# Windowed attention and a gated expert on one core: weights converted 1024 columns at a time, in borrowed memory

## The chip, the core and the metric

The kernel runs on one core of a Trainium2 chip. The core has a matrix engine (TensorE, PE in the rows; PEld is its loading of weights), a vector engine (VectorE, DVE), a scalar engine (ScalarE, ACT), a general one (GpSimd, POOL) and SyncE (SP), which here only issues DMAs. Each runs its own list of instructions in order, and they wait for each other through semaphores. The metric is the device time of one execution in microseconds; less is better. A profile is one more execution, taken by the hardware profiler.

## The reference

Eight batches of attention over 8 heads, 576 positions, 64 numbers a head. Then a gated expert with a convolution over the positions:

```
scores = q @ k.T / 8;  heads 0-3 see the last 32 positions,
                       heads 4-7 every 4th of the last 128
attn   = softmax(scores) @ v;  x = attn, heads side by side (576 x 512 a batch)
h      = relu(x @ w_in)                                   # 512 -> 1024
conv   = sum of conv_w[k] * h at position + k - 1,  k = 0..2
out    = (h * sigmoid(conv)) @ w_out                      # 1024 -> 512
```

All inputs and the output are fp32. The weights reach the device as raw 64-bit words, as the host has them, and are made into fp32 terms there.

## The kernel before

**Numbers.** An expert matmul runs in fp32r, one pass. So that its result is good enough, each operand is a sum of two terms, hi and lo, and a product is three matmuls: hi x hi, hi x lo, lo x hi (`TERMS`). This holds for x (`x0a`, `x0b` are hi and lo of one slot), for w_in (`wi`), for w_out (`wo`) and for the gated h (`g`).

**Attention.** A pair of heads is one attention block, four to a batch, 32 in all. One block is: 36 or 40 small score matmuls (L322, S below); maxima, exp and sums on VectorE and ScalarE; a transpose on VectorE (L369); 42 or 44 matmuls with v (L380, V below); and the copy of the result into hi and lo of x (L432 ScalarE, L435 VectorE). In the first seven blocks (`EASED`) TensorE adds the mask by matmuls (L309), and exp is nine small instructions (L346).

**Expert.** For each batch the first product (L460, E below) makes 16 units of 12 matmuls: 8 pieces of 128 columns of h, each in halves of 288 positions. ScalarE applies relu (L467). The gate of a piece is a scaled copy (L478), two taps (L472 VectorE), sigmoid (L483), the product (L485), and the split into hi and lo of g (L488, L490). The second product (L502, G below) takes blocks of 128 positions, 24 matmuls each, over the 8 pieces.

**Weights.** `weights` loads one chunk of 512 words (L529, half a MiB) and makes its terms. ScalarE takes the magnitude (L538), VectorE shifts it, adds the sign, cuts off the last bits and forms the rest (L540, L542, L545, L547). There are 8 chunks of w_in, 8 of w_out and one small one of conv_w. In ten of the 16 (`SUMMED`) lo comes from TensorE: identity times the main part, minus the rest, minus hi (L556 to L558, one after the other in a PSUM bank; this is called a correction below), and a copy out (L561). In the other six VectorE adds and subtracts (L563, L569).

**Order.** `Planner` writes all engines' orders. Every piece of work has an engine, a cost, a due number (`DUE`, `PAIR`, `WI`, `WO`, `EXTRA`, and `SHIFT` for single tasks), the tasks it comes after and the buffers it uses. At each step the planner takes the engine whose next work can start first by its costs, and among the work that can start within 0.25 of that, the one with the smallest due number. The order is then written out and kept. Where the plan leaves TensorE idle in its first 60 us, `filled` puts in filler matmuls of `ones` with itself (L600), whose result nobody reads. `ones` is the bf16 identity: GpSimd makes an fp32 identity, ScalarE copies it (L573), and the first filler waits for that.

**Buffers.** `qk` has two slots, `v` three, `u` ten, `g` eight (one for each 128 columns of h), and the conversion has four of raw words, three of terms (`w`) and two of rests (`r`). SP issues all loads in the planned order; a load whose slot is still read waits on SP, and what stands behind it waits too.

Of the kernel before, what the change touches and what calls it, by code (L numbers as in the profile page):

```python
# [8 lines left out]
F32 = mybir.dt.float32  # L9
# [27 lines left out]
    0: (508.06, 118.7, 1183.15, 74.57, 324.56, -13.54),  # L37
    1: (77.62, 987.7, -1760.76, 250.32, 1004.25, 273.69),
    2: (-1800.55, 209.28, 1068.97, 212.32, 742.18, 600.16),
    3: (430.32, 309.56, 279.83, 495.43, 968.39, -311.64),  # L40
    4: (-1333.76, -56.0, 788.64, 898.23, 629.43, 69.23),
    5: (-209.08, -1085.66, 3838.62, 239.71, 685.35, 49.23),
    6: (-1730.83, 900.6, 769.13, -1140.48, 291.43, -1030.59),
    7: (249.67, -1019.42, -1317.3, 803.1, 449.65, -1107.9),
}
PAIR = {
    0: (-1284.89, -2039.18, -1339.23, -1351.72),
    1: (-1032.27, -1049.19, -1041.5, -1122.07),
    2: (-994.96, -257.3, -37.45, -138.07),
    3: (88.07, -10.86, -134.77, 220.53),  # L50
    4: (646.12, 416.46, 324.57, 690.94),
    5: (847.1, 778.65, -227.72, 874.3),
    6: (752.11, 349.59, 1190.92, 1132.25),
    7: (3817.41, 1342.98, 1934.23, 391.1),
}
WI = (91.3, 189.33, 106.05, 82.13, -1680.2, -142.95, -815.76, 129.17)
WO = (-809.27, 346.83, 388.99, -762.3, 778.33, 873.39, 232.39, 1087.63)
EXTRA = (-1465.48, 232.79, -92.67, 599.5, 258.06, 231.57, 708.35, -1147.4, -1135.53, -1294.92, -1448.95,
    300.52, 3695.3, 609.75, 18.47, 85.79, -1136.82, 113.69, -959.95, -186.62, 253.06, 28.17, 459.74, -1675.04,
    1.22, -1061.9, 64.19, -192.43, -1248.75, -17.19, -998.69, 3818.85, 955.89, -1328.81, 709.92)  # L60

SHIFT = {
# [11 lines left out]
MASKS = 70.0  # L74


EASED = range(7)
EARLY = (0, 3)
SUMMED = (0, 1, 3, 4, 5, 6, 7, 11, 12, 14)
LEFT = 16  # L80
# [133 lines left out]
def attn_moe(ctx: ExitStack, tc: tile.TileContext, qk_p, qk_d, v_p, v_d, w_in, w_out, conv, mask, out):  # L214
# [306 lines left out]
    def weights(src, n, due, dst=None, pair=None, summed=False):  # L521
# [43 lines left out]
        if dst is not None:  # L565
            return last
# [126 lines left out]
```

## Time and profile before

| | us |
|---|---|
| three runs | 524.24, 525.31, 522.60; median 524.24 |
| profiled execution | 522.08 |
| its span, first to last instruction | 520.3 |
| TensorE busy | 507.4 |
| VectorE busy | 392.0 |
| ScalarE busy | 297.6 |
| DMA queue of SP | 51.10 MB, 29.8% of the span's capacity |

A busy share is an average over the whole span. The granted clock of TensorE is 1.00 of full speed in every slice. DMA is busy mainly in the first 60 us: the first slices of 13 us move 287, 372, 300 and 170 GB/s, later ones mostly under 150. VectorE is at 0.9 or more of most slices until about 170 us and at 0.2 or less in the last 50. The chain of work that ended last is followed back from the last instruction; a piece of it is a run of instructions of one line, with its start and its length, and what the engine waited for stands in it as DMA, another engine, or "issue" (nothing that the profile shows).

### The profile page before, as it was taken

The numbers are of one execution on the slowest core, as the hardware profiler recorded it, in microseconds if no ns is written. First come the engines' busy times: TensorE is split into PE (matmuls) and PEld (weight loads), VectorE is DVE, ScalarE is ACT, GpSimd is POOL, SyncE is SP. The second block draws the span as 40 slices with busy tenths as digits, with TensorE's granted clock in tenths as the row PEclk, the third lists the DMA queues.
The fourth block names the chain that finished last, engine by engine and source line by source line (L and its number), as shares of the span: only waits on it lengthen the run. The fifth ranks groups of instructions, "written<-read, shape, count | busy, mean of one in ns | idle before, by whom it ended". The sixth has DMA issues, their size and how long they took to land.

```text
span 520.3 us, 17211 instructions
## 1 busy us (share of the span) xinstructions
PE 507.4 (98%) x7700; PEld 440.7 (85%) x7700; DVE 392.0 (75%) x676; ACT 297.6 (57%) x637; POOL 1.4 (0%) x26
## 2 busy tenths in 40 slices
PE   5899999999999999999999999999999999999997
PEld 3568889998877998799977998899789988998885
DVE  5899899999989389999978589878876881772400
ACT  6955897667533487348741476765366632862410
POOL 1000000000000000000000000000000000000000
PEclk9999999999999999999999999999999999999999
DMA  8985643101364113532154113202420011001111
GB/s 287 372 300 170 222 153 117 37 1 41 105 213 144 53 54 87 192 125 64 39 176 144 64 54 125 94 1 70 152 72 1 1 43 42 21 2 40 42 41 59
DMA packets 17274, 52.33 MB, mean 101 GB/s; under 512 B 2096, under 2 KB 2480, under 8 KB 17200
## 3 DMA queue, kind: packets, MB, share of 16 engines
q1 hardware_dynamic: 17056, 51.10, 29.8%
q8 instruction: 60, 0.98, 0.8%
q10 hardware_dynamic: 144, 0.13, 0.1%
q14 instruction: 14, 0.11, 0.1%
HBM read 41.79 MB, written 9.44 MB: 98 GB/s over the span
## 4 chain that ended last, share of the span: by engine, by line
PE 96%; DMA 2%; ACT 1%; issue 0%; DVE 0%; SPq 0%; ACTq 0%
PE banks L502 40%; PE banks L460 39%; PE banks L380 7%; PE banks L322 6%; PE banks L600 2%; PE banks L556 1%; DMA qk<-in_qk_d_dram 1%; DMA qk<-in_qk_p_dram 1%; ACT s L346 1%; PE banks L557 0%; PE banks L558 0%; PE banks L309 0%; SPq L529 0%; DVE m L335 0%; ACT wi L561 0%
## 5 line engine op out<-in xcount | busy, mean ns | idle before, releaser
L472 DVE SCALAR_TENSOR_TENSOR u<-u,conv_sb,u 128x576 f32<-128x576 f32 x128 | 103.5, 817 | 31.2 <-ACT u L478 29.4
L467 ACT ACTIVATE u<-banks 128x288 f32<-128x288 f32 x128 | 51.3, 411 | 53.4 <-PE banks L460 53.2
L485 DVE TENSOR_TENSOR u<-u,u 128x576 f32<-128x576 f32 x64 | 47.8, 756 | 14.6 <-ACT u L483 14.1
L514 ACT COPY u<-banks 128x512 f32<-128x512 f32 (+1 forms) x36 | 20.7, 579 | 58.7 <-PE banks L502 57.7
L460 PE MATMUL banks<-x0a,wi 128*128 128x288 f32 x192 | 54.1, 298 | 0.0
L483 ACT ACTIVATE u<-u 128x576 f32<-128x576 f32 x64 | 42.8, 684 | 19.6 <-DVE u L472 19.3
L478 ACT ACTIVATE u<-u,conv_sb 128x576 f32<-128x576 f32 x64 | 49.6, 778 | 3.0 <-DVE u L485 1.9
L460 PE MATMUL banks<-x2a,wi 128*128 128x288 f32 x160 | 45.1, 299 | 0.0
L460 PE MATMUL banks<-x5a,wi 128*128 128x288 f32 x160 | 44.8, 295 | 0.0
L460 PE MATMUL banks<-x4a,wi 128*128 128x288 f32 x160 | 44.7, 294 | 0.0
L460 PE MATMUL banks<-x3a,wi 128*128 128x288 f32 x160 | 44.7, 298 | 0.0
L380 PEld LDWEIGHTS banks<-pt,v 32*64 32x64 f32 x2752 | 34.9, 131 | 10.8 <-issue 4.8
L380 PE MATMUL banks<-pt,v 32*64 32x64 f32 (+2 forms) x2752 | 38.7, 226 | 1.4 <-ACT wi L561 1.1
L322 PEld LDWEIGHTS banks<-qk 64*32 64x32 f32 x2432 | 28.8, 106 | 10.6 <-issue 4.1
L322 PE MATMUL banks<-qk 64*32 64x64 f32 x2432 | 34.2, 226 | 2.1 <-DMA qk<-in_qk_d_dram 0.9
L460 PEld LDWEIGHTS banks<-x0a,wi 128*128 128x128 f32 x192 | 36.0, 188 | 0.2
L360 ACT ACTIVATE s<-s 128x576 f32<-128x576 f32 x25 | 17.1, 686 | 28.2 <-DVE s L358 28.1
L460 PEld LDWEIGHTS banks<-x2a,wi 128*128 128x128 f32 x160 | 29.9, 188 | 0.8 <-ACT u L467 0.2
L460 PEld LDWEIGHTS banks<-x3a,wi 128*128 128x128 f32 x160 | 29.8, 188 | 0.6 <-ACT u L467 0.2
L460 PEld LDWEIGHTS banks<-x5a,wi 128*128 128x128 f32 x160 | 30.0, 188 | 0.2
L460 PEld LDWEIGHTS banks<-x4a,wi 128*128 128x128 f32 x160 | 30.0, 188 | 0.0
L502 PE MATMUL banks<-wo,g0a 128*128 128x512 f32 x72 | 29.1, 404 | 0.0
(139 smaller groups left out, 1283.3 us busy)
## 6 DMA issues: line engine op xcount, KB each, us to landing
qk<-in_qk_d_dram SPq DMA_DIRECT2D x16, 672.0 KB, 4.5
qk<-in_qk_p_dram SPq DMA_DIRECT2D x16, 592.0 KB, 4.7
out_dram<-u SPq DMA_DIRECT2D x31, 256.0 KB, 2.2
v<-in_v_p_dram SPq DMA_DIRECT2D x16, 384.0 KB, 3.6
v<-in_v_d_dram SPq DMA_DIRECT2D x16, 384.0 KB, 3.6
raw<-in_w_out_dram SPq DMA_DIRECT2D x8, 512.0 KB, 3.7
raw<-in_w_in_dram SPq DMA_DIRECT2D x8, 512.0 KB, 6.6
out_dram<-u SPq DMA_DIRECT2D x9, 128.0 KB, 2.3
```

The source lines that it names most:

```text
L322: nc.tensor.matmul(banks[quad * 32:quad * 32 + 32, at[bank], c * W:c * W + W], q, k, start=i == 0 and not eased, stop=i == len(parts) - 1, ...
L360: last = plan.add("ACT", 0.685, step[3], lambda: nc.scalar.activation(out=nine(s.t), in_=nine(s.t), func=AF.Exp, scale=SCALE), [last], [s] ...
L380: nc.tensor.matmul(banks[hd * 64:hd * 64 + 64, bank, o:o + n], v.t[quad * 32:quad * 32 + 32, block // 2, block % 2 * 64:block % 2 * 64 + 6 ...
L460: nc.tensor.matmul(bank(ps)[:, 0:HALF], wi[jw][fc][:, k * 128:k * 128 + 128], x[k].t[jx][:, hf * HALF:hf * HALF + HALF], start=(k == 0 and ...
L467: relu.append(plan.add("ACT", 0.4, due + 1.6 * u + relued, lambda fc=fc, hf=hf, ps=ps: nc.scalar.activation(out=h[fc].t[:, 1 + hf * HALF:1 ...
L472: nc.vector.scalar_tensor_tensor(out=body(c[fc]), in0=h[fc].t[:, k:S + k], scalar=conv_sb[:, k, fc:fc + 1], in1=body(c[fc]), op0=ALU.mult, ...
L478: t = plan.add("ACT", 0.777, d, lambda fc=fc: nc.scalar.activation(out=body(c[fc]), in_=body(h[fc]), func=AF.Copy, scale=conv_sb[:, 1, fc: ...
L483: t = plan.add("ACT", 0.686, d + shaped, lambda fc=fc: nc.scalar.activation(out=body(c[fc]), in_=body(c[fc]), func=AF.Sigmoid), [t], [c[fc ...
L485: t = plan.add("DVE", 0.755, d + times, lambda fc=fc: nc.vector.tensor_tensor(out=body(c[fc]), in0=body(c[fc]), in1=body(h[fc]), op=ALU.mu ...
L502: nc.tensor.matmul(bank(ps), g[k].t[jg][:, col:col + 128], wo[jw][k], start=(k == 0 and i == 0), stop=(k == NF - 1 and i == 2))
L514: t = plan.add("DVE" if half else "ACT", 0.16 + 0.00093 * (c1 - c0), out_due + by_block * u + copied, lambda ps=ps, o=o, c0=c0, c1=c1, cop ...
L600: nc.tensor.matmul(banks[:, i], ones, ones.unsqueeze(1).to_broadcast([128, 4, 128]), start=True, stop=True)
```

## The change

Weights are loaded and converted in eight chunks of 1024 words (one MiB) and not sixteen of 512; one chunk holds two of the former, side by side, and the host's layout follows. A summed chunk is corrected in two halves on TensorE, as a bank holds 512. Four of the eight chunks are summed.

The conversion gets hardly any memory of its own. A `Slot` is a place with two lives: first fp32 scratch (`before`), then the final tile. Magnitude and rest of a chunk stand where its hi will be, and its main part where its lo will be, or in the one `w` where VectorE makes lo. The raw words of w_in are loaded into the places of g, which is not in use yet; those of w_out have one raw buffer. g has four places for pairs of chunks. u grows from 10 to 13.

GpSimd makes the bf16 identity directly and first, then the fp32 one. All eight blocks of the first two batches are eased, a third block's scores use the expert's banks (`EARLY`), and all due numbers are new, `SHIFT` is empty.

```diff
-    0: (508.06, 118.7, 1183.15, 74.57, 324.56, -13.54),
+    0: (1422.91, 1408.33, 435.35, 42.62, 1436.64, -870.71),
...
-EASED = range(7)
-EARLY = (0, 3)
-SUMMED = (0, 1, 3, 4, 5, 6, 7, 11, 12, 14)
+EASED = range(8)
+EARLY = (0, 3, 7)
+SUMMED = (1, 3, 5, 6)
...
-NU, NX, NR, NW, NT = 10, 7, 4, 3, 2
+NU, NX, NR, NW, NT = 13, 7, 1, 1, 2
...
-    wi = [[const.tile([128, 512], F32R, name=f"wi{j}{c}") for c in range(NF)] for j in range(2)]
-    wo = [[const.tile([128, DM], F32R, name=f"wo{j}{c}") for c in range(NF)] for j in range(2)]
+    twice = ctx.enter_context(tc.tile_pool(name="twice", bufs=1))
+
+    class Slot:
+
+        def __init__(self, name, shape, before):
+            self.name, self.shape, self.kept = name, shape, None
+            self.before = twice.tile(before, F32, name=f"{name}early", tag=name)
+
+        def __getitem__(self, at):
+            if self.kept is None:
+                self.kept = twice.tile(self.shape, F32R, name=self.name, tag=self.name)
+            return self.kept[at]
+
+    wi, wo = ([[Slot(f"{n}{j}{c}", [128, 1024], [128, 1024]) for c in range(NF // 2)] for j in range(2)] for n in ("wi", "wo"))
...
-    slots("g", NF, [128, S + REST], F32R, 2)
+    plan.pool("g", [Slot(f"g{i}", [128, 2, 2, S + REST], [128, 2048]) for i in range(NF // 2)])
...
-    def weights(src, n, due, dst=None, pair=None, summed=False):
+    def weights(src, n, due, pair, summed=False, words=None):
+
         f = n / 512
-        raw, u, t = Buffer("raw"), Buffer("w", 1), Buffer("w")
-        r = Buffer("r") if summed else u
-        both = lambda: raw.t[:, :2 * n].bitcast(I32).rearrange("p (n t) -> p n t", t=2)
+        hi, lo = pair
+        raw = words or (Buffer("raw") if n > 512 else None)
+        r, w = [Buffer("r")] if summed else [], [] if summed or n < 512 else [Buffer("w")]
+        u = lambda d=F32: (hi.before if n > 512 else hi).bitcast(d)
+        t = lambda d=F32: (w[0].t if w else lo.before if n > 512 else lo).bitcast(d)
+        both = lambda: (raw[0].t.before if words else raw[0].t if raw else conv_raw)[:, :2 * n].bitcast(I32).rearrange("p (n t) -> p n t", t=2)
...
-            part = plan.add("ACT", 0.62, due + EXTRA[22], lambda: nc.scalar.copy(out=hi, in_=words(t)), [main], [t])
+            part = plan.add("ACT", 0.16 + 0.465 * f, due + EXTRA[22], lambda: nc.scalar.copy(out=hi[:, :], in_=t()), [last])
...
+            halves, added = [slice(0, 512), slice(512, 1024)], []
+            pss = [Buffer("nn" if words else "mm") for _ in halves]
+            for at, ps in zip(halves, pss):
+                added.append(plan.add("PE", 1.43, due + EXTRA[23], lambda at=at, ps=ps: add(ps, at), [part, whole, negated], [*r, ps], "E"))
...
-    made = plan.add("POOL", 0.6, -1e4, lambda: make_identity(nc, ident))
-    made = plan.add("ACT", 0.29, -1e4, lambda: nc.scalar.copy(out=ones, in_=ident), [made])
-    plan.add("ACT", 0.29, -1e4, lambda: nc.scalar.mul(out=minus, in_=ident, mul=-1.0), [made])
+    made = plan.add("POOL", 0.6, -2e4, lambda: make_identity(nc, ones))
+    whole = plan.add("POOL", 0.6, -1e4, lambda: make_identity(nc, ident), [made])
+    negated = plan.add("ACT", 0.29, -5e2, lambda: nc.scalar.mul(out=minus, in_=ident, mul=-1.0), [whole])
...
+    wired = sum([weights(w_in[c], 1024, WI[c], (wi[0][c], wi[1][c]), c in SUMMED, gs[0][c]) for c in range(NF // 2)], [])
+    wored = sum([weights(w_out[c], 1024, WO[c], (wo[0][c], wo[1][c]), c + NF // 2 in SUMMED) for c in range(NF // 2)], [])
```

How this moves instructions is seen best in three places. The numbers behind names are the buffers' own in each program, and line numbers from L300 on differ by 1 to 7 between the two.

SP's first loads, before (the raw words of a chunk go to a `raw` buffer; 128x1024 words of four bytes are half a MiB):

```order
L529 DMA raw_156<-in_conv_dram 128x48
L529 DMA raw_157<-in_w_out_dram 128x1024
L571 DMA kinds_sb<-in_mask_dram 128x320
L294 DMA qk_99<-in_qk_p_dram 128x1184
L529 DMA raw_158<-in_w_in_dram 128x1024
L294 DMA qk_100<-in_qk_d_dram 128x1344
L529 DMA raw_159<-in_w_out_dram 128x1024
L294 DMA qk_99<-in_qk_d_dram 128x1344
L529 DMA raw_156<-in_w_in_dram 128x1024
L294 DMA qk_100<-in_qk_p_dram 128x1184
```

and after (`g0early` is g's place 0 in its first life):

```order
L576 DMA kinds_sb<-in_mask_dram 128x320
L535 DMA conv_raw<-in_conv_dram 128x48
L295 DMA qk_88<-in_qk_p_dram 128x1184
L295 DMA qk_89<-in_qk_p_dram 128x1184
L535 DMA g0early<-in_w_in_dram 128x2048
L297 DMA v_90<-in_v_p_dram 128x768
L295 DMA qk_88<-in_qk_d_dram 128x1344
L295 DMA qk_89<-in_qk_d_dram 128x1344
L297 DMA v_91<-in_v_p_dram 128x768
L535 DMA raw_135<-in_w_out_dram 128x2048
L295 DMA qk_88<-in_qk_d_dram 128x1344
L295 DMA qk_89<-in_qk_p_dram 128x1184
```

Four weight chunks of half a MiB stood among the first nine loads, two of them ahead of the second qk load. Now two qk loads come first, then one MiB of w_in, and the first chunk of w_out only behind four qk and two v loads.

TensorE around the first expert matmul, before (L556 to L558 are a correction, L460 E, L380 V, L600 a filler):

```order
L600 MATMUL banks<-ones 128x512
L556 MATMUL banks<-w_161,ident 128x512
L557 MATMUL banks<-r_163,minus 128x512
L558 MATMUL banks<-wi_72,minus 128x512
L460 MATMUL banks<-x2a,wi_70 128x288
L460 MATMUL banks<-x2b,wi_70 128x288
L460 MATMUL banks<-x2a,wi_78 128x288
L380 MATMUL banks<-pt_114,v_101 64x64 x24
L380 MATMUL banks<-pt_114,v_101 64x32 x8
L380 MATMUL banks<-pt_114,v_101 64x16 x8
L380 MATMUL banks<-pt_114,v_101 64x32 x4
L600 LDWEIGHTS ones
```

and after (the same are L559 to L561, L463, L381 and L607):

```order
L607 MATMUL banks<-ones 128x512
L559 MATMUL banks<-wi13early,ident 128x512
L560 MATMUL banks<-r_137,minus 128x512
L561 MATMUL banks<-wi_580,minus 128x512
L381 MATMUL banks<-pt_102,v_92 64x64 x24
L381 MATMUL banks<-pt_102,v_92 64x32 x8
L381 MATMUL banks<-pt_102,v_92 64x16 x8
L381 MATMUL banks<-pt_102,v_92 64x32 x4
L607 LDWEIGHTS ones
L607 MATMUL banks<-ones 128x512
L463 MATMUL banks<-x0a,wi_580 128x288
L463 MATMUL banks<-x0b,wi_580 128x288
```

Before, the correction above is the fifth, and the first three E stand between it and the fourth V block. After, the one above is the second half of the first chunk, and the third V block and a filler stand between it and the first E. Ahead of these rows there are 39 fillers before and 57 after.

VectorE in its first conversions, before (L540 to L547 are a chunk's steps, L335 to L339 the maxima of an S block):

```order
L540 TENSOR_SCALAR w_162<-w_162 128x512
L542 SCALAR_TENSOR_TENSOR w_160<-raw_157,w_162 128x512
L545 TENSOR_SCALAR w_162<-w_160 128x512
L547 SCALAR_TENSOR_TENSOR r_163<-raw_157,w_162 128x512
L335 TENSOR_REDUCE m_107<-banks 128x2x4
L337 TENSOR_REDUCE m_107<-banks 128x1
L339 TENSOR_SCALAR m_107<-m_107 128x9
L540 TENSOR_SCALAR w_161<-w_161 128x512
L542 SCALAR_TENSOR_TENSOR w_162<-raw_158,w_161 128x512
L545 TENSOR_SCALAR w_161<-w_162 128x512
L547 SCALAR_TENSOR_TENSOR r_164<-raw_158,w_161 128x512
```

and after (L546 to L550 the steps, L336 to L340 the maxima, L365 to L368 an S block's division):

```order
L336 TENSOR_REDUCE m_98<-banks 128x2x4
L338 TENSOR_REDUCE m_98<-banks 128x1
L340 TENSOR_SCALAR m_98<-m_98 128x9
L336 TENSOR_REDUCE m_96<-banks 128x2x4
L338 TENSOR_REDUCE m_96<-banks 128x1
L340 TENSOR_SCALAR m_96<-m_96 128x9
L546 TENSOR_SCALAR wi03early<-wi03early 128x1024
L548 SCALAR_TENSOR_TENSOR wi13early<-g0early,wi03early 128x1024
L365 TENSOR_SCALAR z_101<-z_101 128x9
L367 RECIPROCAL z_101<-z_101 128x9
L368 TENSOR_TENSOR s_95<-s_95,z_101 128x576
L550 TENSOR_SCALAR wi03early<-wi13early 128x1024
```

The maxima of four S blocks now stand ahead of the first weight chunk's first step, where two whole chunks stood around the first block's maxima.

## Rows read from the trace of the kernel before

**Rows 1.** The page: busy engines; DMA issues (count, KB each, us to landing)
```profile
PE 507.4 (98%) x7700; PEld 440.7 (85%) x7700; DVE 392.0 (75%) x676; ACT 297.6 (57%) x637; POOL 1.4 (0%) x26
...
qk<-in_qk_d_dram SPq DMA_DIRECT2D x16, 672.0 KB, 4.5
```

**Rows 2.** TensorE's waits, whole span: waiter, awaited, us in total, times, longest
```profile
PE banks L600 <- ACT ones L573: 5.8, 1, 5.8
PE banks L380 <- ACT wi L561: 1.1, 1, 1.1
PE banks L322 <- DMA qk<-in_qk_d_dram: 0.9, 1, 0.9
```

**Rows 3.** The chain that ended last: start us, us, what, instructions
```profile
2.12 5.23 DMA qk<-in_qk_p_dram
...
8.81 6.37 DMA qk<-in_qk_d_dram
...
21.78 2.91 PE banks L600 x13
24.69 0.86 PE banks L556 x2
25.55 0.23 PE banks L557
...
36.01 0.40 PE banks L460 x3
36.41 1.19 PE banks L380 x72
37.59 0.32 PE banks L600
37.91 1.98 PE banks L460 x15
...
40.55 0.65 issue
...
54.05 1.06 PE banks L322 x65
...
67.68 3.39 PE banks L460 x24
...
96.00 2.76 PE banks L502 x12
...
103.26 5.47 PE banks L502 x24
```

**Rows 4.** Timeline, 0 to 30 us: start, us, engine, line, operation
```profile
1.67 0.29 POOL masks.py:199 TENSOR_SCALAR_AFFINE_SELECT ident<-ident 128x128 f32<-128x128 f32 x1
...
3.10 0.18 DVE L542 SCALAR_TENSOR_TENSOR w<-raw,w 128x24 int32<-128x24 int32 x1
...
9.94 0.31 ACT L346 ACTIVATE s<-banks,m 128x64 f32<-128x64 f32 x1
...
12.47 0.24 ACT L346 ACTIVATION_READ_ACCUMULATOR s<-banks,m 128x1 f32 x1
```

**Rows 5.** Stretches: us, busy us of each engine, clock, DMA share, GB/s
```profile
20.00:25.00 5.00, 4.42 (x100) 2.73 (x100) 4.83 (x14) 5.00 (x25) 0.00 (x0) 1.00 1.00 400
50.00:84.00 34.00, 33.98 (x809) 30.20 (x807) 31.98 (x62) 29.67 (x85) 0.00 (x0) 1.00 0.56 180
```

**Rows 6.** VectorE by line and shape: count, busy us, mean ns, idle before
```profile
L472 DVE SCALAR_TENSOR_TENSOR u<-u,conv_sb,u 128x576 f32<-128x576 f32 x128 | 103.5, 817 | 31.2 <-ACT u L478 29.4
L485 DVE TENSOR_TENSOR u<-u,u 128x576 f32<-128x576 f32 x64 | 47.8, 756 | 14.6 <-ACT u L483 14.1
...
L542 DVE SCALAR_TENSOR_TENSOR w<-raw,w 128x512 int32<-128x512 int32 x16 | 11.0, 686 | 0.3
...
L540 DVE TENSOR_SCALAR w<-w 128x512 int32<-128x512 int32 x16 | 6.6, 416 | 1.8 <-ACT w L538 1.8
```

**Rows 7.** Timeline of VectorE, 112.9 to 115 us
```profile
113.02 2.27 DVE L472 SCALAR_TENSOR_TENSOR u<-u,conv_sb,u 128x576 f32<-128x576 f32 x3
```

More of the change, by code (lines that the diff above doesn't have):

```diff
@@ L544, in weights @@
-        main = last
-        last = step(0.265, [t, u], lambda: nc.vector.tensor_scalar(
-            out=ints(u), in0=ints(t), scalar1=-0x800000, scalar2=None, op0=ALU.bitwise_and))
-        rest = step(0.53, [raw, u, *([r] if summed else [])], lambda: nc.vector.scalar_tensor_tensor(
-            out=r.t if summed else words(r), in0=low().bitcast(U32), scalar=-2.0 ** -52 if summed else 2.0 ** -52,
-            in1=words(u), op0=ALU.mult, op1=ALU.mult))
-        if summed:
-            hi, lo = pair
-            ps = Buffer("nn")
-            part = plan.add("ACT", 0.62, due + EXTRA[22], lambda: nc.scalar.copy(out=hi, in_=words(t)), [main], [t])
-            def add():
-                nc.tensor.matmul(bank(ps), ident, words(t), start=True, stop=False)
-                nc.tensor.matmul(bank(ps), minus, r.t, start=False, stop=False)
-                nc.tensor.matmul(bank(ps), minus, hi, start=False, stop=True)
-            last = plan.add("PE", 1.43, due + EXTRA[23], add, [rest, part], [t, r, ps], "E")
-            return plan.add("ACT", 0.6, due + EXTRA[24], lambda: nc.scalar.copy(out=lo, in_=bank(ps)), [last], [ps])
@@ L562, in weights @@
-        last = rest
-        last = step(0.53, [t, r], lambda: nc.vector.tensor_tensor(
-            out=words(t) if dst is None else dst, in0=words(t), in1=words(r), op=ALU.add))
-        if dst is not None:
-            return last
-        hi, lo = pair
-        last = plan.add("ACT", 0.62, due + EXTRA[22], lambda: nc.scalar.copy(out=hi, in_=words(t)), [last], [t])
-        return step(0.53, [t], lambda: nc.vector.tensor_tensor(out=lo, in0=words(t), in1=hi.bitcast(F32), op=ALU.subtract))
+            out=u(), in_=high().bitcast(F32), func=AF.Abs, scale=2.0 ** -112), [last], raw)
@@ L592, in attn_moe @@
                          [masked[1]])
-    wired = [weights(w_in[c], 512, WI[c], pair=(wi[0][c], wi[1][c]), summed=c in SUMMED) for c in range(NF)]
-    conved = weights(conv, 3 * NF, -9e3, dst=conv_sb.rearrange("p t c -> p (t c)"))
-    wored = [weights(w_out[c], 512, WO[c], pair=(wo[0][c], wo[1][c]), summed=c + NF in SUMMED) for c in range(NF)]
+    gs[0] = [Buffer("g") for _ in range(NF // 2)]
+    flat_conv = conv_sb.rearrange("p t c -> p (t c)")
+    conved = weights(conv, 3 * NF, -9e3, (conv_u, flat_conv))
+    wired = sum([weights(w_in[c], 1024, WI[c], (wi[0][c], wi[1][c]), c in SUMMED, gs[0][c]) for c in range(NF // 2)], [])
+    wored = sum([weights(w_out[c], 1024, WO[c], (wo[0][c], wo[1][c]), c + NF // 2 in SUMMED) for c in range(NF // 2)], [])
     for b in range(B):
```

97 lines of the change are left out of this document (56 added, 41 removed), and 10 rows, old and new, of the table SHIFT.

## The prediction, made before the change was run

> **What bounds the kernel now.** I read the page's busy times first, then who waited for whom on TensorE, then the opening on the timeline, then the chain of work that ended last. TensorE is busy 507.4 of 520.3 us [rows 1]; the reader is to see there that little but TensorE's own work and its early waits is left to change. The longest wait is the 5.8 us before its first instruction, for the bf16 identity that ScalarE copies; the next are 1.1 us for a copy of weight terms and 0.9 us for a load [rows 2]. The last wait in the chain ends at 41.2 us ("issue" [rows 3]); from there on the chain is TensorE alone to the end. Inside TensorE's busy time three things are not the reference's work: 45 filler matmuls (L600), ten corrections of weights (L556 to L558), and the turns between kinds of matmul.
>
> So I compare the two programs by the time at which TensorE has done the same useful work. The scores (S), probability-value products (V), first (E) and second (G) expert products are the same number in both. Their prices are pieces of the chain [rows 3]: an S block 1.06 us; a V block 1.19; 15 E matmuls 1.98, so 0.132 each; 24 G matmuls 5.47, so 0.228 each; 13 fillers 2.91, so 0.224; one filler with the turn around it 0.32; one correction 0.86 + 0.23 + 0.23 = 1.32. After an S or V block the next E pays a turn: 24 E took 3.39 instead of 3.17. There are 64 returns from S or V in both orders, so the turns cancel.
>
> **The change part by part.**
>
> *The identity.* GpSimd's select of the first identity ends at 1.96 us [rows 4]; in the new order it writes the bf16 one first and no ScalarE copy lies between, so fillers start near 2 us instead of 5.8. That alone gives nothing: the first S needs its qk load. This landed at 7.35 (issued 2.12, 5.23 us later [rows 3]) behind 0.55 MB of w_out and conv words. Now only the mask and the conv words stand ahead of it: half a MB less, at 400 GB/s [rows 5], is 1.3 us, and its issue is one DMA earlier, 0.4 us. The first S starts at about 5.7.
>
> *The walk to the first E.* SP gives the loads of S1, S2, 1 MB of w_in and a v, and then waits in order: the third qk load until S1 has read its buffer, the fourth until S2 has. In the same place a qk load of before took 6.37 us from issue to landing [rows 3], and I take 6.4. S1 ends at 6.8; the load issued at 6.9 lands at 13.3. S2 ends at 8.6; the other lands near 15.2. The 17 fillers between are done at 12.7, so S3 runs from 13.3 to 14.5, S4 waits until 15.3 and ends at 16.5. The 18 fillers behind it end at 20.7; S5's load, issued at 14.6, lands at 21.0, and S5 ends at 22.1. Seven fillers; V1 ends at 25.0. Nine exps take 2.8 us (9.94 to 12.71 [rows 4]); those of S5 stand behind VectorE's maxima and V1's x terms, so they run from 27.2 to 30. V2 runs from 27.0 to 28.2, its x terms follow on ScalarE and VectorE until 31.5, V3 ends at 32.7, a filler waits there for the copy of the first correction, and the first E starts at 33.2. Before, it started at 36.0 [rows 3]. First term: -2.8 us. The uncertain number in it is the 6.4 us: at 5, S3 to S5 would be bounded by the fillers and the first E comes 2 us sooner; at 7.5 it comes 2 us later.
>
> *The corrections.* Ten of 512 columns become eight halves of 1024, 2 x 1.32 less in all. But before the first E there were five of the ten and now there are two of the eight (order rows): after it six remain against five. Second term: +1.3 us. The three fewer ahead of it are in the walk.
>
> *Fillers.* 62 for 45, but 57 of them stand before the first E and are in the walk. After it five remain against six. Third term: -0.3 us.
>
> *Width.* On VectorE a two-operand conversion step takes 0.69 us at 512 columns [rows 6] and 0.18 at 24 [rows 4]; 0.16 of it does not grow, and I estimate 1.21 at 1024; one-operand steps go from 0.42 to 0.66. Each pair of steps saves 0.16, on VectorE and ScalarE, which lie beside TensorE: directly I give it nothing. What it can cost is its grain: a TensorE block that waits for x, or an exp, stands behind a step of 1.2 us and not 0.7. From the walk after the first E: V5 waits 0.5 us for the x terms of V4, which stand behind three such steps; S7 waits 1.0 us for exps that follow a copy of 1024 weights; the long run of E waits 0.2 us for V8's x. That is 1.7 us, in place of the 0.65 us that before lost there ("issue" [rows 3]). Fourth term: +1.05 us. Its bounds are -0.65 (no wait left) and about +3 (each of these waits behind one step more).
>
> *The memory.* Raw words of w_in lie in g, terms in the place of the finished ones, and raw, w and r have one, one and two buffers. The one raw buffer makes SP wait for a conversion before each later w_out load, and loads of qk and v and stores queue behind it. The last of these waits is for VectorE's 172nd instruction, near 102 us; the qk loads of the next two S blocks are issued before it, and that is the cover. The g pieces are freed by pairs of chunks; every G block reads all of them anyway. The u buffers go from 10 to 13. I cost all this at nothing; without the cover one late S or V costs TensorE about its own length, 1 us.
>
> A rule of the Trainium skill ("DMA: Bandwidth & Descriptors", section Bandwidth) speaks for the wide loads: transfers should be batched to 1 MiB and more to come near peak, and the fit in its section on the anatomy of one DMA is 2.0 us plus the bytes at 436 GB/s. Estimated from that page, 16 weight loads would be 51 us of queue and 8 would be 35. By the row the queue moved 400 GB/s at a busy share of 1.00 with pieces of half a MiB [rows 5], so the fixed part is already hidden, and the sum takes nothing from it.
>
> *Later.* At the first G of the new order all corrections, 11 S, 8 V and 384 E are done. From 49.5 us, after S7, there are until then 336 E (44.5 us), four S, three V, four corrections, two fillers and seven turns, 59.9 us, and 0.2 of wait: 109.6. Before began G at 96 [rows 3] and mixed it with E. What is left behind that point is the same work in both, and before records no wait in it.
>
> Sum: -2.8 + 1.3 - 0.3 + 1.05 = -0.75 us. The profiled execution took 522.08 us, 1.8 around its span, so such an execution would take 521.3. The median of the runs is 524.24, 2.2 above the profiled one, and I forecast against the median: **523.5 us**. About 0.5%, 2.6 us, is what a measurement of this kernel can tell from no change.
>
> **The rivals.**
>
> *The early loads land in time: faster.* If the qk loads land 5 us after issue instead of 6.4 and the grain costs nothing, the first E comes at 31.2 and no wait follows: -4.8 + 1.3 - 0.3 - 0.65 = -4.5, 519.8 us. For it: over the whole program such a load takes 4.5 us [rows 1]. Against it: from 20 to 25 us the queue is still full [rows 5]. The skill's rule above would work in this way, too. Chance 0.30.
>
> *VectorE is late at the first G: slower.* Now 198 E come in one run and then G, whose first block needs the low part of a w_out chunk, VectorE's 182nd instruction. Between the state at 49 us and it stand 85 instructions: 25 taps of 0.817, 19 products of 0.756 [rows 6], 15 steps of 1024 (15.5 us) and S and V work of 11.4: 61.6 us in durations. Three taps in a row took 2.27 and not 2.45 [rows 7], 7% less, so 57.3 us against TensorE's 60.1. It decides once VectorE's waits pass 2.8 us; from 50 to 84 us before it stood idle 2.0 of 34 [rows 5], which is 3.5 in 60. With twice that G waits 4.2 us there and about 1 us more at the next w_out chunk: -0.75 + 5.2 = +4.5, 528.7 us. Against it: the steps of 1024 are fewer, so fewer of them can wait. Chance 0.22.
>
> *The edits cancel.* The first S comes sooner, but S4 and S5 wait for their loads and the corrections are only put off: the forecast, within 0.5% on either side. Chance 0.48.
>
> **How the numbers follow.** Faster by over 0.5%: 0.30; within: 0.48; slower: 0.22. The likeliest case's own range is 521.6 to 526.8; over all cases it is 518.8 to 528.8, a little beyond the prices of both rivals.
>
> **What would show it.** In the profile after: the first filler near 2 us and the first S near 5.7; waits of S3 to S5 for qk between 12 and 21; the first E between 31 and 35; no TensorE wait over 1.5 us after 50; the first G near 110 with none for VectorE. A wait of over 2 us at the first G, or waits that go on after 130, would make the forecast wrong on the slow side; S3 to S5 without waits for loads on the fast one.

## The result, and the profile after

The changed kernel takes 526.09 us (median of 8 runs, 524.83 to 527.21) against 523.39 of the kernel before (8 runs). The ratio is 1.005, 95% interval [1.003, 1.007]: slower by about 2.6 us, where 523.5 and "no change" was forecast. A second set of six runs (after_again below) gave 526.76 and 1.0074 [1.0059, 1.0089]. The profiled execution took 526.32 us, its span 524.6 (before: 522.08 and 520.3); the granted clock of TensorE is 1.00 in both.

The page after, answering to [rows 1]: TensorE is busy 3.1 us longer with 14 matmuls more, and the qk loads land a little faster over the whole program.

```profile
PE 510.5 (97%) x7714; PEld 442.1 (84%) x7714; DVE 389.1 (74%) x638; ACT 304.9 (58%) x641; POOL 2.0 (0%) x34
...
qk<-in_qk_d_dram SPq DMA_DIRECT2D x16, 672.0 KB, 4.1
```

TensorE's waits after, answering to [rows 2] (waiter, awaited, us in total, times, longest). The wait for the first identity went from 5.8 to 1.3 us. What is new is "issue", time in which TensorE waited for nothing that the profile shows: 5.9 us by this view's rounding, where before had 0.9.

```profile
PE banks L381 <- issue: 2.8, 2, 1.9
PE banks L607 <- issue: 2.2, 1, 2.2
PE banks L607 <- POOL ones masks.py:199: 1.3, 1, 1.3
PE banks L323 <- DMA qk<-in_qk_d_dram: 1.1, 1, 1.1
PE banks L463 <- issue: 0.9, 1, 0.9
PE banks L381 <- DVE x1b L436: 0.6, 1, 0.6
PE banks L463 <- DVE x0b L436: 0.5, 1, 0.5
```

The chain that ended last, after, in the opening, answering to [rows 3] (start us, us, what). S is line 323, V 381, E 463, G 505, a filler 607.

```profile
1.63 4.19 DMA qk<-in_qk_p_dram
...
7.24 6.44 DMA qk<-in_qk_d_dram
...
17.07 2.17 issue
19.25 3.61 PE banks L607 x16
...
29.20 0.83 PE banks L381 x43
30.03 1.95 issue
31.98 0.55 PE banks L381 x19
...
34.24 0.68 DVE x1b L436 x2
...
42.77 0.82 issue
43.58 1.04 PE banks L381 x65
...
88.17 25.70 PE banks L463 x191
113.88 17.70 PE banks L505 x78
```

The reader is to see three things. The first S load lands at 5.82 and the third takes 6.44 us, as forecast. The stalls named "issue" fall among fillers, in the middle of V2, among E matmuls and in the middle of a later V block, where a wait for data would be looked for ahead of a block. And G starts at 113.88, where the forecast had 109.6: 4.3 of the 5.05 us by which the span is longer than forecast (524.6 for 519.55) are lost ahead of it.

TensorE's timeline after, 13 to 45 us (start, us, engine, line, operation; in brackets the idle time ahead):

```profile
13.73 1.13 PE L323 MATMUL banks<-qk 64*32 64x64 f32 x80 [1.05 <-DMA qk<-in_qk_d_dram]
...
19.25 3.61 PE L607 MATMUL banks<-ones 128*128 128x512 bf16 x16 [2.17 <-issue]
...
23.04 1.13 PE L323 MATMUL banks<-qk 64*32 64x64 f32 x80
...
31.98 0.47 PE L381 MATMUL banks<-pt,v 32*64 32x64 f32 x28 [1.95 <-issue]
...
36.12 0.48 PE L463 MATMUL banks<-x0a,wi 128*128 128x288 f32 x1
...
38.00 0.29 PE L463 MATMUL banks<-x1a,wi 128*128 128x288 f32 x1 [0.86 <-issue]
...
43.58 1.02 PE L381 MATMUL banks<-pt,v 32*64 32x64 f32 x69 [0.82 <-issue]
```

Where the stalls stand is the clue. Cut the time at their ends and count TensorE's matmuls and weight loads. The columns are the stretch, its length, the busy us and the count (x) of TensorE's matmuls, of its weight loads, of VectorE, ScalarE and GpSimd, then granted clock, DMA share and GB/s:

```profile
0.00:19.20 19.20, 14.23 (x351) 8.19 (x352) 9.97 (x27) 12.41 (x61) 2.00 (x34) 1.00 0.88 324
19.20:31.95 12.75, 10.68 (x255) 6.14 (x254) 8.61 (x17) 9.20 (x44) 0.00 (x0) 1.00 0.95 364
31.95:37.95 6.00, 4.60 (x127) 3.31 (x128) 5.36 (x11) 4.88 (x13) 0.00 (x0) 1.00 0.60 193
37.95:43.55 5.60, 4.64 (x127) 4.04 (x127) 4.75 (x9) 1.64 (x3) 0.00 (x0) 1.00 0.82 307
```

Between them lie 509, 255 and 254 instructions: two, one and one times 256, less one to three records. The kernel before has the same grid: its stalls at 30.8 and 41.2 stand after 1210 instructions and 510 later, and 703 + 509 = 1212. Its rows:

```profile
0.00:30.75 30.75, 22.22 (x605) 13.58 (x605) 23.47 (x59) 23.59 (x99) 1.36 (x26) 1.00 0.90 332
30.75:41.15 10.40, 9.76 (x255) 7.32 (x255) 9.40 (x19) 5.48 (x11) 0.00 (x0) 1.00 0.72 248
```

Short windows of the DMA view show what ends such a stall. There is no packet of the instruction queue, q8, from 29.20 to 29.45; there is one of 16 KB from 29.45 to 30.45; and TensorE goes on at 31.98.

```profile
## 3 DMA queue, kind: packets, MB, share of 16 engines
q1 hardware_dynamic: 90, 0.27, 80.7%
q8 instruction: 1, 0.02, 6.6%
```

So TensorE's program comes in pages of 16 KB, 256 instructions. A page's transfer starts only after the page ahead of it was entered: in after 2.8, 4.5, 3.4, 3.7 and 3.2 us after (pages entered from 14 to 38 us), 1.1 and 0.7 us for the next two. TensorE runs on 2.3 to 2.5 us after the start. A page of S and V matmuls is used up in 2.6 to 3.8 us, since one S block is 160 instructions in 1.1 us; whenever that is less than the 3.1 to 6.9 us that the next page takes, TensorE stalls.

The Trainium skill ("Runtime: NRT & Kernel Launch", section Instruction fetch mechanics) says that instructions are refilled in blocks of 16 KiB, 256 instructions, and that crossing into a new block is mostly hidden. The trace agrees with the size; here the crossing is not hidden, 5.8 us in four stalls.

### The profile page after: what moved, and what is told of

Same layout as the page of the kernel before. It is cut to its first block, busy times and chain, and to the rows that moved or that the text cites. A ratio compares the mean times of both kernels' runs of the same rounds, so it can differ in the third digit from the quotient of the medians.

```text
span 524.6 us, 17168 instructions
## 1 busy us (share of the span) xinstructions
PE 510.5 (97%) x7714; PEld 442.1 (84%) x7714; DVE 389.1 (74%) x638; ACT 304.9 (58%) x641; POOL 2.0 (0%) x34
## 4 chain that ended last, share of the span: by engine, by line
PE 86%; DVE 7%; DMA 3%; issue 2%; ACT 1%; SPq 0%; DVEq 0%; ACTq 0%
PE banks L505 39%; PE banks L463 34%; PE banks L381 6%; PE banks L323 5%; DMA qk<-in_qk_p_dram 2%; DVE u L475 1%; DMA qk<-in_qk_d_dram 1%; PE banks L607 1%; ACT s L347 1%; DVE pt L370 1%; DVE u L488 1%; DVE m L336 0%; DVE s L368 0%; DVE g L493 0%; DVE x0b L436 0%
## 5 line engine op out<-in xcount | busy, mean ns | idle before, releaser
L505 PE MATMUL banks<-wo,g 128*128 128x512 f32 x864 | 207.6, 395 | 0.0
L505 PEld LDWEIGHTS banks<-wo,g 128*128 128x128 f32 x864 | 159.1, 188 | 34.2
L463 PE MATMUL banks<-x0a,wi 128*128 128x288 f32 x224 | 63.7, 299 | 0.0
L493 DVE TENSOR_TENSOR g<-u,g 128x576 fp32r<-128x576 f32 x64 | 45.5, 751 | 13.8 <-ACT g L491 13.7
L463 PE MATMUL banks<-x3a,wi 128*128 128x288 f32 x192 | 54.6, 300 | 0.0
L491 ACT CAST g<-u 128x576 fp32r<-128x576 f32 x64 | 42.1, 675 | 15.7 <-PE banks L505 11.9
L381 PEld LDWEIGHTS banks<-pt,v 32*64 32x64 f32 x2752 | 34.8, 131 | 13.6 <-issue 7.5
L463 PE MATMUL banks<-x5a,wi 128*128 128x288 f32 x160 | 45.0, 296 | 0.0
L463 PE MATMUL banks<-x6a,wi 128*128 128x288 f32 x160 | 45.0, 296 | 0.0
L463 PEld LDWEIGHTS banks<-x0a,wi 128*128 128x128 f32 x224 | 42.2, 188 | 1.4 <-issue 1.0
L381 PE MATMUL banks<-pt,v 32*64 32x64 f32 (+2 forms) x2752 | 38.9, 226 | 3.6 <-issue 2.8
L463 PEld LDWEIGHTS banks<-x3a,wi 128*128 128x128 f32 x192 | 36.2, 189 | 0.5
L463 PE MATMUL banks<-x2a,wi 128*128 128x288 f32 x128 | 35.9, 296 | 0.0
L463 PE MATMUL banks<-x0b,wi 128*128 128x288 f32 x112 | 33.2, 296 | 0.5 <-DVE x0b L436 0.5
```

Of the source, the lines that this page charges most:

```text
L381: nc.tensor.matmul(banks[hd * 64:hd * 64 + 64, bank, o:o + n], v.t[quad * 32:quad * 32 + 32, block // 2, block % 2 * 64:block % 2 * 64 + 6 ...
L463: nc.tensor.matmul(bank(ps)[:, 0:HALF], wi[jw][fc // 2][:, fc % 2 * 512 + k * 128:fc % 2 * 512 + k * 128 + 128], x[k].t[jx][:, hf * HALF:h ...
L491: hi = plan.add("ACT", 0.675, d + split, lambda fc=fc: nc.scalar.copy(out=gate(fc, 0), in_=body(c[fc])), [t, *(read[b - 1, fc] if b % 2 el ...
L493: lo = plan.add("DVE", 0.755, d + rest, lambda fc=fc: nc.vector.tensor_tensor(out=gate(fc, 1), in0=body(c[fc]), in1=gate(fc, 0).bitcast(F3 ...
L505: nc.tensor.matmul(bank(ps), g[k].t[:, k % 2, jg, col:col + 128], wo[jw][k // 2][:, k % 2 * 512:k % 2 * 512 + 512], start=(k == 0 and i == ...
```

## The experiments

**Theory A:** pages come late while the load queue is full, and TensorE's new order uses them up faster. **Theory B:** ScalarE's and VectorE's 1024-wide steps deliver exps and x terms late. **Theory C:** the data loads land late in their new order. "Page stall" is an "issue" stall at a page's end. Times are medians, with the ratio to the runs of before on the same chip.

**More instructions for the same columns.** The first eight fillers of after are cut into 4 (shift48) or 8 (shift112) matmuls each.

```
+        if filled_so_far[0] <= 8:
+            for c in range(4):       # 8, of 64 columns, in shift112
+                nc.tensor.matmul(banks[:, i, c * 128:c * 128 + 128], ones, ones[:, 0:128], start=True, stop=True)
+            return
```

> Theory A (TensorE's instructions come in pages of 256 and a page comes late while the load queue is full): the same columns in 48 more instructions (24 matmuls, 24 weight loads) put each page's end 48 instructions earlier in the useful work. The four 'issue' stalls of after (2.17 at 17.1, 1.95 at 30.0, 0.86 at 37.1, 0.82 at 42.8 us) stay at TensorE instructions 705, 1217, 1473 and 1729, so they stand before other matmuls: the one inside V2 comes after 32 of its matmuls, not after 56. Their sum stays within 4 to 7 us, the time within 1.5 us of after's 526.1. Theory B (x terms and exps of the 1024-wide steps come late): the stalls stay before the same matmuls (56 into V2) with the same lengths. Theory C (data loads late): the same as B, and the waits named qk stay the only ones that move.

> As the kernel with 48 more instructions, with 112 more. Theory A: the page that ended inside V2 now ends about at V2's first matmul, where TensorE waits for x anyway, so that the stall of 1.95 us shrinks below 1.2 or is merged with that wait; the others move by 112 instructions; sum of 'issue' stalls 3 to 6 us, time 523.5 to 526.5. Theories B and C: the 1.95 us stall stays 56 matmuls into V2.

shift48: 527.74 us, 1.0092 [1.0053, 1.0130]. shift112: 528.02 (the median of seven runs, without one of 533.9), 1.0085 [1.0056, 1.0114]. The stretch up to the first long stall, in shift48:

```profile
0.00:19.50 19.50, 13.41 (x351) 9.88 (x352) 7.63 (x22) 12.60 (x62) 2.00 (x34) 1.00 0.86 322
```

The same in shift112:

```profile
0.00:11.75 11.75, 7.97 (x223) 6.34 (x224) 3.68 (x14) 7.26 (x33) 2.00 (x34) 1.00 0.81 299
```

In shift48 the stall comes again after exactly 703 instructions, though that place is now inside S5 and no longer among fillers; in shift112 one comes at 447, 256 earlier. B and C cannot move a stall by its count. The stall in V2 did not move as expected, it vanished: its page's transfer started 1.1 us after entry. The times were missed, both kernels are slower than expected. In shift112 most fillers behind the stall took 0.43 us each and not 0.22, with a granted clock of 0.75 from 11.75 to 18.5 us, so that half of that stretch ran at 1.2 GHz.

**The kernel before, with more instructions.** 23 of its fillers, each as four matmuls of 128 columns.

```
+        if 13 <= filled_so_far[0] <= 35:
+            for c in range(4):
+                nc.tensor.matmul(banks[:, i, c * 128:c * 128 + 128], ones, ones, start=True, stop=True)
+            return
```

> The kernel before, with 23 of its fillers (those that ran from 21.7 to 29.6 us) each written as four matmuls of 128 columns in place of one of 512: the same columns, 138 more TensorE instructions, nothing else moved. Theory A: a page of 256 instructions must last some 5 to 6 us here (2.4 to 3.6 until its successor's transfer starts, 2.35 from there until it runs), and now pages are used up sooner; stepping through the trace of before with these numbers gives 'issue' stalls of 2.4 near 24.6, and 1.2 each near 36 and 41 us in place of 0.29 and 0.65: 2 to 5 us longer than before. Theory B (grain of the 1024-wide steps) and theory C (data loads): no conversion and no load of this kernel is changed, so within 0.7 us of before.

525.99 us, 1.0040 [1.0019, 1.0062]. No load, no conversion and no order is changed, yet it costs 2.1 us, nearly what the whole change costs; the profiled spans are 522.7 and 520.3, both at a granted clock of 1.00. In the profile the correction that ran at 24.69 [rows 3] waits until 27.06, after 956 instructions (703 + 253), and the page's packet starts at 24.74. The profile names x0b there: it ended at the same moment by chance, and in before this correction ran ahead of x0b. B and C fall as the only cause. The other stalls were shorter than stepped. The stretch up to the stall, in before_split:

```profile
0.00:27.00 27.00, 17.53 (x478) 11.86 (x478) 19.15 (x50) 21.18 (x94) 1.36 (x26) 1.00 0.89 336
```

And the correction behind it, on TensorE's timeline:

```profile
27.06 1.12 PE L556 MATMUL banks<-w,ident 128*128 128x512 f32 x2 [1.86 <-DVE x0b L435]
```

**No fillers, and the identity alone.**

```
-FILLED = 60.0
+FILLED = 0.0
```

> The 62 filler matmuls are left out (their results are used by nothing): about 114 TensorE instructions fewer ahead of the first E. Theory A: the page ends stand about 34, 100, 114 and 114 instructions later in the useful work, and each page is asked for earlier against the end of its predecessor, since TensorE waits for data instead of running fillers; the 'issue' stalls sum to under 4 us and stand before other matmuls. The granted clock in the opening is lower, which costs up to 8 us; time 522 to 532. Theory B: stalls of the same lengths at the same useful matmuls. Theory C: stalls as before, qk waits longer by what the fillers filled.

528.5 us, 1.0095 [1.0060, 1.0129]. Missed: the page stalls did not fall under 4 us. There are two in the opening, 5.65 us in sum (5.80 in after), and one of 1.15 at 172.6 us. Without fillers S5 and V1 follow so closely that a page lasts 2.4 us, and the one behind it is waited for 3.74 us. Fewer instructions do not help where the rest come faster. The run is no test of the pages alone: in its opening TensorE also waits longer for loads and exps, and the granted clock is 0.66 from 45 to 50 us.

```
-    made = plan.add("POOL", 0.6, -1e4, lambda: make_identity(nc, ident))
-    made = plan.add("ACT", 0.29, -1e4, lambda: nc.scalar.copy(out=ones, in_=ident), [made])
+    made = plan.add("POOL", 0.6, -2e4, lambda: make_identity(nc, ones))
+    whole = plan.add("POOL", 0.6, -1e4, lambda: make_identity(nc, ident), [made])
```

> The kernel before with one part of the change alone: GpSimd writes the bf16 identity first, and ScalarE's copy is gone; nine more fillers are placed in the time won, and a w_in load and a v load change places. The first S still waits for its load at 7.4 us. Theory A: about 20 more TensorE instructions ahead of 10 us move every page end by 20; the two stalls stay near 30 and 41 us, 0.5 to 1.5 us in sum: within 1 us of before. Theories B and C: the same within 1 us.

523.51 us, 1.0012 [0.9983, 1.0042]: this part alone changes nothing that can be measured. Its profile is of its slowest run, with a granted clock of 0.52 from 10 to 15 us and the first S at 8.89, so the places of its stalls are not compared.

**Fewer bytes, or later ones.** light leaves parts of the early qk and v loads out; late_wo moves one load; late_thin also drops 16 fillers; paced also puts the last MiB of w_in behind a v load.

```
+        moved = {id(loads[7]): starts[id(loads[1])] - 1e-3}    # late_wo
+        moved = {id(loads[7]): starts[id(loads[1])] - 1e-3, id(loads[2]): vs[4] + 1e-3}    # paced
+        order = sorted(((moved.get(id(t), s), t) for s, t in order), key=lambda x: x[0])
```

> The qk and v loads of the first two batches into a buffer that was already filled move only 16 new columns, or the first of six pieces of v (the rest of these buffers holds older data); all instructions of the engines and their order stay. Theory A: the instruction pages no longer stand behind full load queues; the 'issue' stalls fall from 5.8 us in sum to under 1.5, the qk waits (1.5 us) go too, the first E starts at 30 to 33 instead of 36.1, the time is 519 to 522 us. Theory B: the stalls stay (5 to 6 us), 524.5 to 526. Theory C: the qk waits of 1.5 us go, and with them whatever came late behind them, but the 'issue' stalls stay at their matmuls with their lengths: 523.5 to 525.

> After, with one load moved: the first 1 MiB of w_out is issued just ahead of the second MiB of w_in (near 16.9 us) and not at 9.56, so it no longer stands ahead of S5's qk load. No engine's order changes but SP's. Theory A: with less in the load queues from 10 to 17 us the page wanted at 17.1 starts sooner (1.1 to 2 us after the page before it was entered, not 2.77), the stall of 2.17 falls to about 1, S5 starts near 21.2 behind the same 16 fillers, and all behind it comes 1 to 2 us sooner, except that the queue is then fuller from 17 to 30 and gives some back in the stall near 30: 524 to 526. Theory C: S5's load lands near 18.7 and not 21.1, and the stalls keep their lengths: S5 at 23, no gain, 526. Theory B: no change before V1, x terms of V2 as late as before, 526.

> As the kernel with the moved load, and without 11 of the 18 fillers ahead of S5 and 5 of the 7 ahead of V1 (32 TensorE instructions fewer). Theory A: S5 starts at 19 to 20, V1 at 21 to 23, the page ends fall 22 to 32 instructions later in the useful work, first E at 33 to 35 (36.1 in after), time 522.5 to 525; part of the gain comes back as longer 'issue' stalls behind V1, since the pages still cannot come faster than one in about 6 us. Theory B: V1 to V3 wait for x terms and exps as long as before, named DVE and ACT, and take back what S5 gains: 526.

> As the kernel with the first w_out load moved to 16.6 us (late_wo), and the last MiB of w_in is issued behind the v load of about 30 us and not at 25. Nothing else moves. Theory A: less of the queue is full from 26 to 36 us, so the pages entered at 23.7 and 29.2 us are followed by a transfer in 1 to 2.5 us and not in 2.96 and 4.45; the stalls near 29 and 36 us (0.28 and 1.09) fall to under 0.5 in sum, TensorE passes the state of after's first G about 1 us sooner than late_wo did (111.6): 522.5 to 524.5. Theory C: the same loads are only later, none of them was waited for: no change against late_wo, 524 to 525.

light: 524.10 us, 1.0017 [0.9995, 1.0039]; late_wo: 524.14, 1.0034 [1.0001, 1.0066]; late_thin: 525.43, 1.0038 [1.0014, 1.0063]; paced: 525.17, 1.0043 [1.0022, 1.0063]. Only late_wo lies in the range that theory A gave it; the other three are slower. In light the page stalls fell to 4.0 us and not under 1.5: SP only brought the w_in loads forward, so the queue was full again from 25 to 30 us, where the page stall of 2.4 us stayed; from 30 to 35, with the queue nearly idle, the stalls at the next pages were gone:

```profile
25.00:30.00 5.00, 2.67 (x63) 1.47 (x60) 3.99 (x8) 4.21 (x21) 0.00 (x0) 1.00 0.99 397
30.00:35.00 5.00, 4.29 (x126) 3.10 (x127) 4.23 (x9) 3.42 (x9) 0.00 (x0) 1.00 0.15 49
```

In late_wo the stall of 2.17 fell to 0.32, the first E came at 33.84 (36.12 in after) and the first G at 111.6, against C, which had S5 stay at 23. In the profiles of paced and late_thin no page stall is left, and G starts at 111.0. Yet their medians are not measurably below that of after. TensorE's longest waits in late_thin show part of the reason; no "issue" is among them:

```profile
PE banks L565 <- ACT wi L560: 1.5, 1, 1.5
PE banks L323 <- DMA qk<-in_qk_d_dram: 1.5, 2, 1.3
PE banks L616 <- POOL ones masks.py:199: 1.4, 1, 1.4
PE banks L381 <- DVE x0b L436: 1.0, 1, 1.0
PE banks L310 <- ACT s L347: 0.9, 1, 0.9
PE banks L616 <- ACT s L347: 0.8, 1, 0.8
PE banks L381 <- ACT s L347: 0.8, 1, 0.8
```

There TensorE was busy 5.97 of the 10 us from 20 to 30, and in the next 10 the granted clock was 0.72 on average, so that over half of that stretch ran at 1.2 GHz:

```profile
20.00:30.00 10.00, 5.97 (x228) 3.86 (x223) 7.55 (x15) 7.31 (x31) 0.00 (x0) 0.94 1.02 416
30.00:40.00 10.00, 10.00 (x207) 7.83 (x206) 8.80 (x16) 7.18 (x19) 0.00 (x0) 0.72 0.84 332
```

The granted clock goes along with the times, and no run separates it from the rest. Its mean over the span is 0.993 in the median run of late_thin and 0.995 in that of paced, against 0.999 and 1.000 in the runs of before beside them; 0.005 of a span of 522 us is about 5 us at 1.2 GHz in place of 2.4. The seven runs of paced at 0.995 or more have a median of 523.91, the five below it 525.74; of before on the same chip, fifteen at 0.995 or more have 522.40, and two at 0.993 took 525.30 and 525.41.

ScalarE and VectorE stand right behind the pages. In paced ScalarE waits 2.80 us for the load that was moved, and V1's x terms are queued behind it. So one of the moved loads now comes late, which theory C did not expect (ScalarE's timeline):

```profile
24.81 1.16 ACT L549 ACTIVATE wo02early<-raw 128x1024 f32<-128x1024 f32 x1 [2.80 <-DMA raw<-in_w_out_dram]
25.87 1.03 ACT L561 CAST wi<-wi13early 128x1024 fp32r<-128x1024 f32 x1
26.80 0.68 ACT L435 CAST x0a<-banks 128x256 fp32r<-128x256 f32 x2
```

**Other orders.** weights_later plans anew with rules for SP; x_first is paced with conversion steps moved behind x terms; after_again is after, beside x_first.

```
+    loads[1].after.append(qk_loads[1, 1])    # weights_later; loads[2], loads[3] too
+    loads[5].after.append(loads[3])          # loads[6] to loads[8] too
...
+        put("ACT", 12, 19)                   # x_first: Abs of w_out behind the casts of x1
+        put("DVE", 41, 48)                   # its steps behind x1b; six more moves, and a w_out load later
```

> After, planned anew with three rules for SP: the second to fourth MiB of w_in only behind S6's qk load, and all of w_out behind the third of w_in; dues, costs and widths are those of after. The w_out conversion then stands behind the x terms of V1 to V4 on ScalarE and VectorE and no longer ahead of them (order of the program). Theory A with ScalarE and VectorE next behind: the sum of the 'issue' stalls ahead of 60 us falls from 5.8 to under 2.5, the 1 us that V2 waited for x in late_wo goes too, first E at 31.5 to 33.5; the time is 520.5 to 523.5, under after by 3 to 5, about that of before. Theory B alone (grain): the first E comes 1 us sooner at most, the stalls stay over 4 us: 524 to 526. If the conversions put off are missed later, VectorE is waited for at the first G (near 108 us), and the gain comes back there.

> As the paced kernel, with the same loads and the same TensorE order; on ScalarE four 1024-wide Abs steps, and on VectorE the four steps of the first w_out chunk, stand behind the x terms of the next V blocks and no longer ahead of them. In the paced kernel TensorE had no page stall over 0.3 us, but waited 4.7 us ahead of 50 us for exps and x terms that stood behind a ScalarE step which waited up to 2.8 us for its own load. Theory A alone (pages were all of the loss): nothing left to win, as the paced kernel, G begins at 111, 525. Theory A with B next behind: x0b, the exps of S6 and x1b come 1 to 1.8 us sooner, first E at 32.5 to 33.5 (34.5 in the paced kernel), the first G at 109 to 110.3, 522 to 524.5, under after by 2 to 4; part may come back as page stalls, since pages are then used up faster.

> The kernel after unchanged, on the same chip as the kernel with x terms first, so that the two are compared with the same runs of before: 524.8 to 527.2 as in its first runs, with 'issue' stalls of 4 to 7 us in its profile at TensorE instructions 705, 1217, 1473 and 1729 again (theory A), since their places hang on the count of instructions alone and their lengths on the loads.

weights_later: 530.07 us, 1.0144 [1.0119, 1.0169], a miss: page stalls of 1.3 and 2.5 us stayed, x and exps were waited for longer, and the first E came at 39.6. x_first: 526.49, 1.0080 [1.0058, 1.0101]; after_again: 526.76, 1.0074 [1.0059, 1.0089], with 5.2 us of page stalls, this time at two of the four places.

after_again is the program of after, yet its first E came at 38.36 and not 36.12: its two stalls were longer (2.83 and 2.40 us), and the granted clock was 0.66 in the stretch with the second one:

```profile
30.00:40.00 10.00, 7.60 (x166) 5.47 (x155) 7.38 (x14) 7.22 (x27) 0.00 (x0) 0.66 0.57 199
```

So a time out of one profile can differ by 2 us from the next execution's.

x_first missed its range. Its first E came at 32.63, earlier than the 33.2 of the prediction, but V4 and V5 then waited 1.39 and 1.68 us for x2b and x3b, and G began at 112.1. VectorE was full there (x_first, 30 to 40 us):

```profile
30.00:40.00 10.00, 7.81 (x206) 6.29 (x204) 9.56 (x16) 6.88 (x12) 0.00 (x0) 1.00 0.83 266
```

**Pages and conversions crossed.** In after, paced and x_first the first w_out chunk is converted on 32 of its 1024 columns; the other columns' terms are zero.

```
+        w_ = slice(0, few) if few else slice(None)
-            out=u(I32), in0=u(I32), scalar1=3, ...
+            out=u(I32)[:, w_], in0=u(I32)[:, w_], scalar1=3, ...    # and so in all five steps
```

> After, with ScalarE's Abs step and VectorE's four steps of the first w_out chunk done on 32 of its 1024 columns (the rest of its terms is zero, written by GpSimd at the start): 3.1 us less of VectorE and 1 us less of ScalarE ahead of the first G, most of it between 20 and 36 us; loads and TensorE's order stay. Theory A (pages bind here): page stalls of 4 to 6 us stay, first E at 35 to 38, time within 1.2 us of after (525 to 527). Theory B (the 1024-wide conversions bind): x terms and exps come 1 to 3 us sooner, the first G at 110 to 112, 523 to 524.5.

> The same cut in the paced kernel, which has no page stalls. If pages and conversions bind in turn: the waits for x3b and exps (0.9 and 1.0 us in paced) fall by half or more, first E at 33 to 34.5, G from 109 to 110.5, 522.5 to 524.5, 1 to 2 us under paced; what ScalarE's Abs still waits for its load stays. Theory A alone: as paced, 524.5 to 525.5. Theory B alone: as the cut in after.

> The same cut in the kernel with x terms first, where VectorE was busy 9.56 of the 10 us from 30 to 40 and V4 and V5 waited 1.4 and 1.7 us for x2b and x3b. If the two bind in turn: those two waits go, first E stays at 32.5 to 33, the first G comes at 108.5 to 110, 521.5 to 524, 2.5 to 4 under x_first and after; this is then what after would be without the pages and with room on VectorE, near the forecast. If page stalls come back instead as TensorE runs ahead, 0.5 to 1.5 us of 'issue' per page, 525.

| | whole | cut |
|---|---|---|
| after | 1.0050 [1.003, 1.007], 1.0074 [1.0059, 1.0089] | 1.0069 [1.0045, 1.0094] |
| paced | 1.0043 [1.0022, 1.0063] | 1.0031 [1.0009, 1.0053] |
| x_first | 1.0080 [1.0058, 1.0101] | 1.0028 [1.0011, 1.0046] |

The column of the cut is from one chip, the other from several, and after alone differs by 0.0024 (1.3 us) between its two sets. With that in mind, less conversion is worth nothing in after, 0.6 us and within the intervals in paced, and 2.7 us in x_first, where the waits of V4 and V5 fell from 1.39 and 1.68 to 0.67 and 0.65 us in the profile. This fits two limits that bind in turn: while pages hold TensorE back, conversions have time; once pages come in time, conversions hold it back. For paced it is not shown. In narrow_paced's profile, its slowest run, the wait for x3b did not fall by half: it was 4.15 us (0.90 in paced), since ScalarE waited 4.63 us for the last MiB of w_in, the load that paced issues late, and x3's terms stood behind that step:

```profile
39.93 1.12 ACT L550 ACTIVATE wi01early<-g3early 128x1024 f32<-128x1024 f32 x1 [4.63 <-DMA g3early<-in_w_in_dram]
```

The times of the last two expectations were too low by about 0.5 us; page stalls come back (2.4 us in V2 of narrow_x_first's profile, 1.6 in narrow_paced's). What made the runs of one kernel differ, as paced's from 523.25 to 527.96, no profile shows; the granted clock goes along with it in part, and the two profiles of after show that the page stalls differ as well.

No version is measurably faster than the kernel before.

## Why the prediction was wrong

- **The first S and the loads: right.** First filler at 1.35 (forecast near 2), first S at 5.87 (5.7), S3 at 13.73 (13.3), S4 at 15.40 (15.3). S5's load landed at 21.14 (21.0); the third load took 6.44 us (6.4).
- **The step that failed is the walk to the first E, the first term, -2.8 us.** It measured +0.1: 36.12 after, 36.01 before [rows 3]. The walk gave TensorE every instruction at once. The page stall at 17.07, 2.17 us, put S5 at 23.04, 1.9 us behind its load, since 16 fillers stood between; the one at 30.03, 1.95 us, split V2 and delayed V3. I took the 0.65 us of "issue" in [rows 3] as a wait that those for x and exps would replace. It was the same page grid, and the new order, with corrections moved out and S and V closer together, made it cost 5.8 us in the profile.
- **With shorter page stalls ahead of it** the first E comes at 33.84 (late_wo, 0.6 us of them), 34.46 (paced, none) or 32.63 (x_first, 1.5), around the forecast 33.2. These kernels move loads as well, so this supports the rest of the walk but does not prove it.
- **The fourth term, +1.05, was too small as well.** After the first E the page stalls were 0.86 and 0.82, and 0.7 us was waited for x and exps; the sum, 2.4, stands for the forecast 1.7. In paced the waits for x, exps and weight copies ahead of 50 us are 4.3 us (the expectation for x_first has 4.7, which counts a later one), against 0.6 in after, where TensorE reached most of them later. Part of paced's stands behind ScalarE steps that waited for moved loads.
- **The corrections and fillers** (+1.3 and -0.3) are counts and stand as counted. What is left of the 4.3 us by which the first G is late (113.88 for 109.6), after 2.9 at the first E and 0.7 of waits, is 0.7 us, and 0.75 more is lost behind it; neither was taken apart.
- **Memory: right.** No wait over 0.5 us is shown between 50 and 114 us.
- **The rivals.** "VectorE is late at the first G" gave the right sign by a wrong mechanism: TensorE waits for nothing there. "Early loads land in time" is out, the landing times were as forecast. No case had a wait for the program itself, and slower by over 0.5% had a chance of 0.22. That 526.09 lies inside the range of the likeliest case, 521.6 to 526.8, is luck: its upper end is not worked out (the bounds of the fourth term alone give 521.8 to 525.5), and what filled it are stalls that it did not have.
- Open: what delays a page's transfer. paced has delays of 2.0, 1.9, 1.8 us and nearly none at a queue share of 0.91 to 1.00, after one of 3.6 at 0.74, so the share alone does not decide it. Open too: how much of the 2.6 us between the medians is page stalls. That they cost time by themselves is shown by before_split (2.1 us); paced and late_thin, whose profiles have none, did not get it back in their medians. Not tried: a program whose TensorE instructions are fewer for the same S and V work.

## What to carry to other kernels

A stall called "issue" in the middle of a block is a hint to count instructions: if two such stalls stand a multiple of 256 apart, TensorE waits for its program. Where many small matmuls run while the loads fill the queue, try slow instructions among them (not tried here), and treat a new filler or a split matmul as something that uses up the page. When one such limit goes, look at the next one before counting the gain.

## What the runs showed of the hardware that was not expected

- TensorE's program arrives in 16 KB pages of 256 instructions. A page's transfer starts after its predecessor is entered: over all 17 profiles the median is 2.6 us where the page was entered between 12 and 42 us (93 pages), and 0.8 us after 60 us. TensorE runs on 2.2 to 2.6 us after the start of the transfer if it was waiting.
- A page must so last about 3.2 us where the median is 0.8, and up to 6.9 at the longest delay seen (4.5 + 2.35). S and V pages here last 2.4 to 3.9 us when nothing slow is among them.
- A page stall can carry another name: in before_split the profile put 1.86 us down to x0b, at a page's end.
